# Expert 0's gated output as the accumulator's first value, and the forms of x on VectorE alone

## The chip, the core and the metric

The kernel runs on one core of a Trainium2 chip. TensorE does the matrix products, VectorE and ScalarE read the product banks (PSUM) and write SBUF, GpSimd works from SBUF to SBUF and also issues some transfers, SyncE issues the other transfers. Each engine takes its instructions strictly in the order in which they stand in its queue. The metric is the device time of one launch in microseconds; the median of three runs counts.

## The reference

A recurrent attention gives x (3072 tokens of 384 features). A mixture of 8 experts with a Sinkhorn-normalised gate P follows, and a small gated network after that.

```
P = exp(x @ w_gate - max); 8 times: P /= P.sum(1); P /= P.sum(0); P *= N / E
for e in range(E):
    h = np.maximum(x @ w1[e], 0.0)
    out += P[:, e:e + 1] * (h @ w2[e])
x = out
return ((x @ m1) * (x @ m2)) @ w3 @ w_out
```

The change lies in the sum over the experts: in how the term of expert 0 comes into `out`.

## The kernel before, in words

**Stages.** From 0 to about 430 us the attention runs, and beside it the whole of expert 0 (its raw output, without the gate, goes to DRAM as `y0_d`, three slices `kk` of 128 features each). From there to about 1753 us run experts 1 to 7 in three **passes** of two chunks `s` of 512 tokens. Then comes the gated network. A pass has 14 **units** (expert `e_`, half `h` of its hidden features).

**A unit** (`unit`) has first products and second products. The first products make the hidden features of two pairs `q` of slices by a scheme with 7 multiplications in place of 8 (`STEPS`); their moving operands are not x itself but nine **forms** of it, sums and differences of x's blocks, each split in a high and a low part (`fm(j, 0)`, `fm(j, 1)`, kept in tiles `xT` and `xr`). ScalarE holds partial products in the four buffers `rt` (`hold`), VectorE adds them back into the bank (`done`, rows `b<-b,rt`), ScalarE and VectorE make the high and low part of the positive part (`relu`, tiles `hA`, `hB`). The second products fill six banks, chunk 1 before chunk 0, three slices each; VectorE multiplies each bank by the gate (`tmp<-b,pb`), and GpSimd adds the result to `acc` (six accumulators of 128x512). In the first unit of a pass, (1, 0), VectorE writes `acc` directly.

**Forms** (`forms`). At the end of a pass x of the next two chunks lies in a region of `xT`. ScalarE makes nine high parts; nine low parts (`form`) and four differences (`diff`) are made by VectorE or GpSimd, whichever a planner takes. The differences lie in the four `rt` buffers too.

**Expert 0's term** (`add_first`). At unit (4, 0) of each pass the gate of expert 0 is loaded into an `rt` buffer per chunk, six slices of `y0_d` into the two `tmp` buffers in turn, GpSimd or VectorE multiplies, GpSimd adds to `acc`.

**Beside it** run the loads of the weights (`wA`, `wS`, issued by GpSimd in passes 1 and 2; in pass 0 they are formed from raw weights), and the conversion of the last network's weights (`convert`, tiles `cv`, `cvr`), lowest in priority, on all three vector engines, with loads and stores on SyncE's queue. After a pass `acc` is stored to `xf_d`.

**What sets the order.** Every operation is entered in a list with its priority, cost and dependences, and a planner (`Plan.order`) lays them out in advance on a time line of its own estimates; each engine's queue then follows that line, and no engine steps past a waiting instruction.

Of the kernel before, what the change touches and what calls it, by code (L numbers as in the profile page):

```python
# [334 lines left out]
class Kernel:  # L335
# [634 lines left out]
    def forms(self, p, prio):  # L970
# [22 lines left out]
        def diff(y, a, b, r):  # L993
            g.op(both, lambda e: self.tt(e, tv[y](), a(), b(), ALU.subtract), r=rk + r, w=[t[y]], prio=prio)
# [15 lines left out]
    def unit(self, p, e_, h, pr, pe, pb):  # L1010
# [75 lines left out]
        for s in (1, 0):  # L1086
            bl = [(M[q][3]["12" if s else "11"], M[q][4]) for q in range(2)] + [(M[q][3]["22" if s else "21"], M[q][4] + 1) for q in range(2)]
            pbv = lambda s=s: T["pb"][:, pb[s].at]
            for kk in range(3):
                y = self.psum.new("yb")  # L1090

                def m2(e, y=y, kk=kk, bl=tuple(bl)):
                    o = self.ps(y, 512)
                    for x, (hh, b) in enumerate(bl):
                        hv = self.hv(hh)
                        wh, wl = self.w2(b, 0, kk), self.w2(b, 1, kk)
                        self.mm(o, wh, hv[:, 0], start=(x == 0), stop=False)
                        self.mm(o, wl, hv[:, 0], start=False, stop=False)
                        self.mm(o, wh, hv[:, 1], start=False, stop=(x == 3))
                g.op({"PE": 12 * .229}, m2, r=[(hh, i, 0) for hh, b in bl for i in range(2)] + [("w", b % 8, i) for hh, b in bl for i in range(2)],  # L1100
                     w=[y], prio=pr + .1 + .01 * (3 * (1 - s) + kk))
                av = lambda s=s, kk=kk: T["acc"][:, s, kk]
                ak = ("acc", s, kk)
                if e_ == 1 and h == 0:
                    g.op({"DVE": dveb(512)}, lambda e, y=y, av=av, pbv=pbv: self.tt("DVE", av(), self.ps(y, 512), pbv(), ALU.mult),
                         r=[y, pb[s]], w=[ak], prio=pe)
                else:
                    tm = self.tmpring.new()
                    tv = lambda tm=tm: T["tmp"][:, tm.at]
                    g.op({"DVE": dveb(512)}, lambda e, y=y, tv=tv, pbv=pbv: self.tt("DVE", tv(), self.ps(y, 512), pbv(), ALU.mult),  # L1110
                         r=[y, pb[s]], w=[tm], prio=pe)
                    g.op({"POOL": pool2(512)}, lambda e, tv=tv, av=av: self.tt(e, av(), av(), tv(), ALU.add),
                         r=[tm], w=[ak], prio=pe)
# [3 lines left out]
    def add_first(self, p, pr):  # L1117

        nc, g, T = self.nc, self.g, self.T
        for s, ch in enumerate(self.PASSES[p]):  # L1120
            b = self.rt.new()
            bv = lambda b=b: T["rt"][:, b.at]
            self.dma(bv, lambda ch=ch: T["p_d"][0, 512 * ch:512 * ch + 512].partition_broadcast(128), 262144, ["pd"], [b], pr)
            for kk in range(3):
                tm = self.tmpring.new()
                tv = lambda tm=tm: T["tmp"][:, tm.at]
                self.dma(tv, lambda ch=ch, kk=kk: T["y0_d"][kk, :, 512 * ch:512 * ch + 512], 262144,
                         [("y0", 2 * ch + st, kk) for st in range(2)], [tm], pr)
                g.op({"POOL": pool2(512), "DVE": BB * dveb(512, True)}, lambda e, tv=tv, bv=bv: self.tt(e, tv(), tv(), bv(), ALU.mult), r=[b], w=[tm], prio=pr)
                av = lambda s=s, kk=kk: T["acc"][:, s, kk]  # L1130
                g.op({"POOL": pool2(512)}, lambda e, tv=tv, av=av: self.tt(e, av(), av(), tv(), ALU.add), r=[tm],
                     w=[("acc", s, kk)], prio=pr)

    def phase_b(self):
# [31 lines left out]
        for n, (p, e_, h) in enumerate(units):  # L1166
# [7 lines left out]
            if (e_, h) == (1, 0):  # L1174
                self.forms(p, pr - .6)
            if h == 0:
                pb = [self.pbring.new() for _ in range(2)]
                for s in range(2):
                    self.dma(lambda s=s, pb=pb: T["pb"][:, pb[s].at], lambda s=s, e_=e_, p=p: T["p_d"][
# [7 lines left out]
            if (e_, h) == (4, 0):  # L1187
                self.add_first(p, pr + .6)
            if (e_, h) == (7, 1) and p < 2:
                for s, ch in enumerate(self.PASSES[p]):  # L1190
                    self.dma(lambda ch=ch: T["xf_d"][ch], lambda s=s: T["acc"][:, s], 786432, [("acc", s, kk) for kk in range(3)], [("xf", ch)], 260 + n / 100)

    def spread_p(self):
# [23 lines left out]
        self.after("pd", [g.wr["pd", i] for i in range(2)], -200, hook=free)  # L1217

# [54 lines left out]
    def phase_c(self):  # L1273
# [48 lines left out]
        self.after("yfree", self.e0_ops + [g.wr["lgr", c] for c in range(NCH)], 2999, hook=lambda end: outr.free.extend([(end, i) for i in range(2)]))  # L1322
# [3 lines left out]
        for ci, c in enumerate((5, 4, 0, 1, 2, 3)):  # L1326
# [5 lines left out]
            if ci > 1:  # L1332
                self.dma(xs, lambda c=c: T["xf_d"][c], 786432, [("xf", c)], ak, pc - 1.5)
# [158 lines left out]
```

## Time and profile before

| | us |
|---|---|
| median of three runs | 2114.1 (2111.39 to 2123.24) |
| the profiled execution, its own time | 2105.79 |
| its span, first to last instruction | 2104.0 |
| TensorE busy | 2025.7 |
| VectorE busy | 1230.1 |
| GpSimd busy | 847.2 |
| ScalarE busy | 708.2 |

Busy time is the union of an engine's instructions. "Idle before" in a row is the time that an engine stood still ahead of an instruction, and the name behind the arrow is what ended it. The granted clock of TensorE is 1.00 at 2.4 GHz and 0.50 at 1.2 GHz.

### The profile page before, as it was taken

Reading aid. Unit: us, or ns where it says so; the run is one execution under the profiler, and the core shown is the slowest. Engines: PE = TensorE matmul, PEld = TensorE weight load, DVE = VectorE, ACT = ScalarE, POOL = GpSimd, SP = SyncE. Lnnn points to the kernel's source line nnn. Section 1 sums busy time; section 2 is a strip of 40 time slices with the busy share of each in tenths; the row PEclk is TensorE's granted clock in tenths of the full one; section 3 lists DMA queues with packets and bytes.
Section 4 is the critical chain, followed back from the end, with each engine's and each line's share of the span. In section 5 each row is a group of like instructions: output and inputs, shape, how many; then the busy total and the mean of one; then the engine's idle time right before and its main releaser. Section 6 shows DMA issues by size and latency. Waiting matters only on the chain.

```text
span 2104.0 us, 39081 instructions
## 1 busy us (share of the span) xinstructions
PE 2025.7 (96%) x16017; PEld 1731.0 (82%) x16017; DVE 1230.1 (58%) x1935; ACT 708.2 (34%) x1355; POOL 847.2 (40%) x891
## 2 busy tenths in 40 slices
PE   2899999999999999999999999999999999999999
PEld 1799889988887888788887887888877888988888
DVE  7998883554535535766767767576677543222222
ACT  3543333243433433423322324223333222222222
POOL 3111101257668767544456455344564534200000
PEclk9899999999999999999999999999999999999999
DMA  6533333175546546655555545646555446410000
GB/s 218 163 88 109 94 101 106 56 267 207 194 177 227 186 183 232 235 194 212 210 201 187 192 149 192 235 166 209 194 197 210 157 139 192 99 46 16 16 18 28
DMA packets 165458, 331.57 MB, mean 158 GB/s; under 512 B 13280, under 2 KB 117664, under 8 KB 153760
## 3 DMA queue, kind: packets, MB, share of 16 engines
q1 hardware_dynamic: 131392, 193.82, 27.5%
q0 software_dynamic: 33888, 135.28, 18.7%
q8 instruction: 125, 2.05, 0.4%
q14 instruction: 53, 0.43, 0.1%
HBM read 235.10 MB, written 93.95 MB: 156 GB/s over the span
## 4 chain that ended last, share of the span: by engine, by line
PE 75%; DVE 3%; DMA 2%; issue 1%; POOL 1%; ACT 1%; SPq 0%; DVEq 0%; POOLq 0%; ACTq 0%
PE b L357 75%; DMA wA<-wq_d 1%; DMA wo_d<-cv 1%; DVE cv L371 1%; DVE xr L368 0%; DVE b L368 0%; POOL acc L368 0%; POOL cv L368 0%; DVE hA L371 0%; DMA rawB<-in_moe_w 0%; POOL tmp L368 0%; POOL wA L368 0%; ACT rt L361 0%; DVE tmp L368 0%; DMA w_d<-cv 0%
## 5 line engine op out<-in xcount | busy, mean ns | idle before, releaser
L357 PE MATMUL b<-hA,wA 128*128 128x512 f32 (+1 forms) x2367 | 504.6, 353 | 3.5 <-DVE hA L371 3.5
L357 PEld LDWEIGHTS b<-hA,wA 128*128 128x128 f32 x2367 | 391.1, 189 | 65.9 <-DVE hA L371 4.3
L368 POOL TENSOR_TENSOR acc<-acc,tmp 128x512 f32<-128x512 f32 x252 | 330.2, 1313 | 178.2 <-DVE tmp L368 176.7
L357 PE MATMUL b<-hB,wA 128*128 128x512 f32 x1521 | 388.3, 390 | 0.0
L357 PEld LDWEIGHTS b<-hB,wA 128*128 128x128 f32 x1521 | 286.4, 188 | 60.0 <-DVE hB L371 0.4
L357 PE MATMUL b<-xr,wA 128*128 128x256 f32 (+1 forms) x1620 | 328.8, 336 | 3.3 <-DVE xr L368 3.1
L368 DVE TENSOR_TENSOR tmp<-b,pb 128x512 f32<-128x512 f32 x234 | 161.2, 689 | 231.6 <-PE b L357 211.6
L357 PEld LDWEIGHTS b<-xr,wA 128*128 128x128 f32 x1620 | 250.6, 190 | 36.7 <-DVE xr L368 3.5
L361 ACT ACTIVATE rt<-b 128x512 f32<-128x512 f32 x300 | 178.0, 597 | 247.1 <-PE b L357 238.9
L357 PE MATMUL b<-xT,wA 128*128 128x512 f32 x1008 | 250.7, 389 | 0.6 <-DMA wA<-wq_d 0.6
L368 DVE TENSOR_TENSOR b<-b,rt 128x512 f32<-128x512 f32 x252 | 173.2, 695 | 110.8 <-ACT rt L361 69.8
L357 PEld LDWEIGHTS b<-xT,wA 128*128 128x128 f32 x1008 | 188.9, 188 | 40.8 <-DMA wA<-wq_d 1.4
L368 POOL TENSOR_TENSOR cv<-cv 128x256 f32<-128x256 f32 (+3 forms) x171 | 124.9, 730 | 197.7 <-DVE cv L1254 114.3
L357 PE MATMUL b<-xT,wS 128*128 128x512 f32 x756 | 199.5, 390 | 4.6 <-ACT rt L361 4.6
L371 DVE SCALAR_TENSOR_TENSOR hA<-b,hA 128x512 fp32r<-128x512 f32 x215 | 144.3, 687 | 67.3 <-ACT hA L1060 40.8
L357 PEld LDWEIGHTS b<-xT,wS 128*128 128x128 f32 x756 | 141.5, 188 | 35.9 <-ACT rt L361 6.7
L368 DVE TENSOR_TENSOR rt<-b,rt 128x512 f32<-128x512 f32 x48 | 33.2, 692 | 186.0 <-PE b L357 186.0
L1060 ACT ACTIVATE hB<-b 128x512 fp32r<-128x512 f32 x169 | 100.4, 595 | 96.6 <-DVE b L368 94.7
L371 DVE SCALAR_TENSOR_TENSOR hB<-b,hB 128x512 fp32r<-128x512 f32 x169 | 115.0, 684 | 26.4 <-ACT hB L1060 26.0
L361 ACT ACTIVATE cv<-cv 128x256 fp32r<-128x256 f32 x72 | 29.1, 404 | 284.9 <-DVE cv L371 284.9
L1060 ACT ACTIVATE hA<-b 128x512 fp32r<-128x512 f32 x167 | 97.6, 596 | 47.6 <-DVE b L368 26.1
L368 POOL TENSOR_TENSOR wA<-rawB,wA 128x768 fp32r<-128x768 f32 (+1 forms) x53 | 91.1, 1729 | 31.8 <-ACT wA L361 27.2
(175 smaller groups left out, 2355.9 us busy)
## 6 DMA issues: line engine op xcount, KB each, us to landing
wA<-wq_d POOLq DMA_DIRECT2D x56, 1536.0 KB, 9.0
wq_d<-wA SPq DMA_DIRECT2D x28, 1536.0 KB, 7.0
wS<-ws_d POOLq DMA_DIRECT2D x56, 512.0 KB, 4.9
rawB<-in_moe_w SPq DMA_DIRECT2D x108, 192.0 KB, 3.1
ws_d<-wS SPq DMA_DIRECT2D x28, 512.0 KB, 3.2
w_d<-cv SPq DMA_DIRECT2D x112, 128.0 KB, 1.8
pb<-p_d SPq DMA_DIRECT2D x42, 256.0 KB, 3.8
cvr<-in_w3T SPq DMA_DIRECT2D x32, 256.0 KB, 2.7
```

The lines of the kernel that those rows point to most:

```text
L357: self.nc.tensor.matmul(*args, skip_group_check=True, **kw)
L361: self.nc.scalar.activation(out=out, in_=in_, func=AF.Copy, **({} if scale is None else {"scale": scale}))
L368: self.E[eng].tensor_tensor(out=out, in0=in0, in1=in1, op=op)
L371: self.nc.vector.scalar_tensor_tensor(out=out, in0=in0, scalar=scalar, in1=in1, op0=op0, op1=op1)
L1060: g.op({"ACT": actb(512)}, lambda e: nc.scalar.activation(out=hv(0), in_=self.ps(s, 512), func=AF.Relu), r=[s], w=[(out, 0, 0)], prio=pe)
```

## The change

`add_first` is gone. A new `first` runs at the start of a pass, ahead of unit (1, 0): per chunk it loads the gate of expert 0 into a buffer of the ring `pb`, loads the slices of `y0_d` straight into `acc`, and VectorE multiplies `acc` by the gate in place. Unit (1, 0) then goes through `tmp` and GpSimd's addition like every other unit. The ring `pb` has a third buffer, which lies in `yr` (expert 0's output tile, free after expert 0). The forms' low parts and differences are VectorE's alone. The store of `acc` after a pass is cut into six of 256 KB, one for each slice, so that a slice's load can follow its own store.

```diff
-        both = {"POOL": pool2(512), "DVE": dveb(512, True)}
+        dve_ = {"DVE": dveb(512)}
...
-            g.op(both, lambda e: self.tt(e, four(self.fm(j, 1)), src(), four(self.fm(j, 0).bitcast(F32)), ALU.subtract),
+            g.op(dve_, lambda e: self.tt("DVE", four(self.fm(j, 1)), src(), four(self.fm(j, 0).bitcast(F32)), ALU.subtract),
...
-            g.op(both, lambda e: self.tt(e, tv[y](), a(), b(), ALU.subtract), r=rk + r, w=[t[y]], prio=prio)
+            g.op(dve_, lambda e: self.tt("DVE", tv[y](), a(), b(), ALU.subtract), r=rk + r, w=[t[y]], prio=prio)
...
-                if e_ == 1 and h == 0:
-                    g.op({"DVE": dveb(512)}, lambda e, y=y, av=av, pbv=pbv: self.tt("DVE", av(), self.ps(y, 512), pbv(), ALU.mult),
-                         r=[y, pb[s]], w=[ak], prio=pe)
-                else:
-                    tm = self.tmpring.new()
...
-    def add_first(self, p, pr):
...
+    def first(self, p, pr):
+
+        g, T = self.g, self.T
+        pb = [None, None]
+        for s in (1, 0):
+            ch = self.PASSES[p][s]
+            b = pb[s] = self.pbring.new()
+            bv = lambda b=b: self.pv(b)
+            self.dma(bv, lambda ch=ch: T["p_d"][0, 512 * ch:512 * ch + 512].partition_broadcast(128), 262144, ["pd"], [b], pr)
             for kk in range(3):
...
+                self.dma(av, lambda ch=ch, kk=kk: T["y0_d"][kk, :, 512 * ch:512 * ch + 512], 262144,
+                         ["bopen"] + [("y0", 2 * ch + st, kk) for st in range(2)], [("acc", s, kk)], pr)
+                g.op({"DVE": dveb(512)}, lambda e, av=av, bv=bv: self.tt("DVE", av(), av(), bv(), ALU.mult), r=[b], w=[("acc", s, kk)], prio=pr)
...
+            if (e_, h) == (1, 0):
+                self.first(p, pr - .5)
...
-            if (e_, h) == (4, 0):
-                self.add_first(p, pr + .6)
...
-                for s, ch in enumerate(self.PASSES[p]):
-                    self.dma(lambda ch=ch: T["xf_d"][ch], lambda s=s: T["acc"][:, s], 786432, [("acc", s, kk) for kk in range(3)], [("xf", ch)], 260 + n / 100)
+                for s in (1, 0):
+                    ch = self.PASSES[p][s]
+                    for kk in range(3):
+                        self.dma(lambda ch=ch: T["xf_d"][ch, :, kk], lambda s=s, kk=kk: T["acc"][:, s, kk], 262144, [("acc", s, kk)],
+                                 [("xf", ch, kk)], 260 + n / 100)
```

The planner lays out the rest anew. Three places follow, all at the change from pass 0 to pass 1; `b` is a product bank, the names are those above.

VectorE during the first products of unit (7, 1). Before:

```order
L371 SCALAR_TENSOR_TENSOR hB<-b_137,hB 128x512
L371 SCALAR_TENSOR_TENSOR hB<-b_135,hB 128x512
L368 TENSOR_TENSOR b_134<-b_134,rt 128x512
L368 TENSOR_TENSOR b_139<-b_139,rt 128x512
L368 TENSOR_TENSOR xr<-xT,xr 128x512
L371 SCALAR_TENSOR_TENSOR hB<-b_134,hB 128x512
L371 SCALAR_TENSOR_TENSOR hA<-b_139,hA 128x512
L371 SCALAR_TENSOR_TENSOR hA<-b_141,hA 128x512
L371 SCALAR_TENSOR_TENSOR hA<-b_136,hA 128x512
```

The same place now:

```order
L371 SCALAR_TENSOR_TENSOR hB<-b_135,hB 128x512
L371 SCALAR_TENSOR_TENSOR hB<-b_138,hB 128x512
L368 TENSOR_TENSOR b_137<-b_137,rt 128x512
L368 TENSOR_TENSOR b_134<-b_134,rt 128x512
L368 TENSOR_TENSOR rt<-xT,rt 128x512
L371 SCALAR_TENSOR_TENSOR hB<-b_137,hB 128x512
L371 SCALAR_TENSOR_TENSOR hA<-b_141,hA 128x512
L371 SCALAR_TENSOR_TENSOR hA<-b_134,hA 128x512
L371 SCALAR_TENSOR_TENSOR hA<-b_136,hA 128x512
L368 TENSOR_TENSOR xT<-xT 128x512
L368 TENSOR_TENSOR xT<-rt,xT 128x512 x2
L368 TENSOR_TENSOR xr<-xT,xr 128x512
```

One operation of the forms stands between the last `done` and the `relu` rows in both; the low part `xr` has moved behind the `relu` rows, together with what was GpSimd's.

VectorE from the fourth gate product of unit (7, 1) into unit (1, 0) of pass 1, now (before, no row on `acc` stood here):

```order
L368 TENSOR_TENSOR tmp<-b_141,pb 128x512
L371 SCALAR_TENSOR_TENSOR cv<-cv 128x256
L368 TENSOR_TENSOR acc<-acc,pb 128x512
L368 TENSOR_TENSOR tmp<-b_134,pb 128x512
L368 TENSOR_TENSOR tmp<-b_136,pb 128x512
L368 TENSOR_TENSOR b_135<-b_135,rt 128x512
L1251 TENSOR_SCALAR cv<-cvr 128x256
L368 TENSOR_TENSOR b_138<-b_138,rt 128x512
L371 SCALAR_TENSOR_TENSOR hB<-b_135,hB 128x512
L368 TENSOR_TENSOR acc<-acc,pb 128x512
L371 SCALAR_TENSOR_TENSOR hA<-b_138,hA 128x512
L368 TENSOR_TENSOR acc<-acc,pb 128x512
```

The first product of `first` stands between the fourth and the fifth gate product of unit (7, 1), the next two among the `done` and `relu` rows of unit (1, 0).

SyncE's queue at the same place. Before:

```order
L388 DMA xT<-xs_d 128x6x128 x4
L388 DMA cvr<-in_moe_w 128x512
L388 DMA w_d<-cv 128x256 x2
L388 DMA pb<-p_d 128x512
L388 DMA xf_d<-acc 128x1536
```

Now:

```order
L388 DMA xf_d<-acc 128x512
L388 DMA xT<-xs_d 128x6x128 x4
L388 DMA acc<-y_d 128x512
L388 DMA xf_d<-acc 128x512
L388 DMA yr<-p_d 128x512
L388 DMA xf_d<-acc 128x512
L388 DMA cvr<-in_moe_w 128x512
L388 DMA w_d<-cv 128x256
L388 DMA xf_d<-acc 128x512
L388 DMA w_d<-cv 128x256
L388 DMA acc<-y_d 128x512 x2
```

`acc<-y_d` is the load of expert 0's slice; the first stands behind the four loads of the next pass's x (`xT<-xs_d`), the second and third behind the store of a converted weight (`w_d<-cv`).

## Rows read from the trace of the kernel before

**Rows 1.** The page's first part: busy time, share of the span, instructions.

```profile
PE 2025.7 (96%) x16017; PEld 1731.0 (82%) x16017; DVE 1230.1 (58%) x1935; ACT 708.2 (34%) x1355; POOL 847.2 (40%) x891
```

**Rows 2.** Busy table: stretch, length, busy PE, PEld, DVE, ACT, POOL, granted clock.

```profile
651.00:667.00 16.00, 13.34 (x58) 10.39 (x58) 6.98 (x10) 7.24 (x14) 13.48 (x11) 1.00 0.41 125
...
851.00:863.00 12.00, 8.91 (x39) 7.08 (x39) 11.12 (x10) 8.38 (x16) 10.42 (x10) 1.00 0.35 127
863.00:1105.00 242.00, 242.00 (x1069) 200.35 (x1069) 163.66 (x273) 76.33 (x146) 116.41 (x131) 1.00 0.60 212
1105.00:1148.00 43.00, 38.84 (x167) 30.40 (x165) 33.99 (x49) 13.88 (x28) 28.16 (x28) 1.00 0.53 174
...
1302.00:1312.00 10.00, 6.51 (x28) 5.08 (x27) 9.93 (x9) 6.44 (x13) 8.03 (x7) 0.97 0.41 141
...
1555.00:1598.00 43.00, 38.59 (x166) 30.51 (x165) 33.59 (x46) 14.14 (x28) 29.92 (x30) 1.00 0.51 176
```

**Rows 3.** TensorE's waits from 360 us on: total us, times, longest.

```profile
PE b L357 <- ACT rt L361: 11.0, 10, 2.1
PE b L357 <- DVE xr L368: 4.0, 2, 3.1
PE b L357 <- DVE hA L371: 3.5, 1, 3.5
```

**Rows 4.** Instructions on tile rt: ns shortest/median/longest, first and last start.

```profile
L368 POOL TENSOR_TENSOR tmp<-tmp,rt x18: 1277/1294/1360, 657.6 to 1574.8; 128x512 f32<-128x512 f32 x18
...
L388 SPq DMA_DIRECT2D rt<-p_d x6: 319/320/978, 630.1 to 1525.1; - x6
...
L368 DVE TENSOR_TENSOR xr<-rt,xr x4: 676/680/1466, 432.3 to 1315.8; 128x512 fp32r<-128x512 f32 x4
```

**Rows 5.** Timeline at the change to pass 1: VectorE, then GpSimd, then TensorE.

```profile
856.22 5.97 DVE L368 TENSOR_TENSOR xr<-xT,xr 128x512 fp32r<-128x512 f32 x1
...
856.66 1.28 POOL L368 TENSOR_TENSOR rt<-xT 128x512 f32<-128x512 f32 x1
857.91 2.51 POOL L368 TENSOR_TENSOR xT<-xT 128x512 fp32r<-128x512 f32 x2
860.39 1.25 POOL L368 TENSOR_TENSOR rt<-xT,rt 128x512 f32<-128x512 f32 x1
...
862.25 0.73 PE L357 MATMUL b<-xr,wA 128*128 128x512 f32 x2 [3.09 <-DVE xr L368]
```

**Rows 6.** The same table as rows 2, behind the wait at pass 2.

```profile
1311.40:1314.70 3.30, 3.30 (x10) 2.54 (x9) 2.93 (x7) 0.00 (x0) 0.31 (x1) 0.50 0.34 123
```

**Rows 7.** Transfers issued from 860 to 875 us: count, KB each, us to landing.

```profile
xT<-xs_d SPq DMA_DIRECT2D x4, 384.0 KB, 6.1
xf_d<-acc SPq DMA_DIRECT2D x1, 768.0 KB, 4.1
```

**Rows 8.** The same from 878 to 900 us.

```profile
wA<-wq_d POOLq DMA_DIRECT2D x2, 1536.0 KB, 11.8
...
xf_d<-acc SPq DMA_DIRECT2D x1, 768.0 KB, 14.7
...
pb<-p_d SPq DMA_DIRECT2D x1, 256.0 KB, 5.1
w_d<-cv SPq DMA_DIRECT2D x2, 128.0 KB, 13.6
```

**Rows 9.** All issues of the page's kind: mid-pass loads of expert 0's slices.

```profile
tmp<-y_d SPq DMA_DIRECT2D x18, 256.0 KB, 3.2
```

**Rows 10.** Timeline at the start of pass 0: GpSimd, then VectorE.

```profile
429.87 3.38 POOL L368 TENSOR_TENSOR wA<-rawB,wA 128x768 fp32r<-128x768 f32 x2 [1.08 <-ACT wA L361]
433.21 3.87 POOL L368 TENSOR_TENSOR wA<-acc,wA 128x768 fp32r<-128x768 f32 x2
...
433.73 1.92 DVE L368 TENSOR_TENSOR wA<-sums,wA 128x128 fp32r<-128x128 f32 x1
435.57 0.69 DVE L368 TENSOR_TENSOR b<-b,rt 128x512 f32<-128x512 f32 x1
```

More of the change, by code (lines that the diff above doesn't have):

```diff
@@ L1087, in unit @@
             bl = [(M[q][3]["12" if s else "11"], M[q][4]) for q in range(2)] + [(M[q][3]["22" if s else "21"], M[q][4] + 1) for q in range(2)]
-            pbv = lambda s=s: T["pb"][:, pb[s].at]
+            pbv = lambda s=s: self.pv(pb[s])
             for kk in range(3):
@@ L1115 @@
-    STEPS = [(q, s) for ss in ((0, 1), (2, 3), (4,), (5,), (6,)) for q in range(2) for s in ss]
-    def add_first(self, p, pr):
-        nc, g, T = self.nc, self.g, self.T
-        for s, ch in enumerate(self.PASSES[p]):
-            b = self.rt.new()
-            bv = lambda b=b: T["rt"][:, b.at]
+                tm = self.tmpring.new()
+                tv = lambda tm=tm: T["tmp"][:, tm.at]
+                g.op({"DVE": dveb(512)}, lambda e, y=y, tv=tv, pbv=pbv: self.tt("DVE", tv(), self.ps(y, 512), pbv(), ALU.mult),
+                     r=[y, pb[s]], w=[tm], prio=pe)
@@ L1123, in add_first @@
+                g.op({"POOL": pool2(512)}, lambda e, tv=tv, av=av: self.tt(e, av(), av(), tv(), ALU.add),
+                     r=[tm], w=[ak], prio=pe)
+    STEPS = [(q, s) for ss in ((0, 1), (2, 3), (4,), (5,), (6,)) for q in range(2) for s in ss]
+    def first(self, p, pr):
[5 more added lines that the diff above has]
+            bv = lambda b=b: self.pv(b)
             self.dma(bv, lambda ch=ch: T["p_d"][0, 512 * ch:512 * ch + 512].partition_broadcast(128), 262144, ["pd"], [b], pr)
@@ L1124, in add_first @@
             for kk in range(3):
[L1125 to L1129, printed above, removed]
                 av = lambda s=s, kk=kk: T["acc"][:, s, kk]
-                g.op({"POOL": pool2(512)}, lambda e, tv=tv, av=av: self.tt(e, av(), av(), tv(), ALU.add), r=[tm],
-                     w=[("acc", s, kk)], prio=pr)
+                self.dma(av, lambda ch=ch, kk=kk: T["y0_d"][kk, :, 512 * ch:512 * ch + 512], 262144,
+                         ["bopen"] + [("y0", 2 * ch + st, kk) for st in range(2)], [("acc", s, kk)], pr)
@@ L1186, in phase_b @@
                 self.after("cv0", [g.wr["acc", 0, 2]], 2)
-            if (e_, h) == (4, 0):
-                self.add_first(p, pr + .6)
             if (e_, h) == (7, 1) and p < 2:
-                for s, ch in enumerate(self.PASSES[p]):
-                    self.dma(lambda ch=ch: T["xf_d"][ch], lambda s=s: T["acc"][:, s], 786432, [("acc", s, kk) for kk in range(3)], [("xf", ch)], 260 + n / 100)
+                for s in (1, 0):
+                    ch = self.PASSES[p][s]
+                    for kk in range(3):
+                        self.dma(lambda ch=ch, kk=kk: T["xf_d"][ch, :, kk], lambda s=s, kk=kk: T["acc"][:, s, kk], 262144, [("acc", s, kk)],
+                                 [("xf", ch, kk)], 260 + n / 100)
     def spread_p(self):
@@ L1217, in spread_p, with pv @@
         self.after("pd", [g.wr["pd", i] for i in range(2)], -200, hook=free)
+        self.after("yrfree", self.e0_ops + [g.wr["lgr", c] for c in range(NCH)], -200, hook=lambda end: self.pbring.free.append((end, 2)))
+    def pv(self, b):
+        return self.T["pb"][:, b.at] if b.at < 2 else self.T["yr"].rearrange("p s n -> p (s n)")[:, 0:512]
     def hv(self, h, part=0, n=512):
@@ L1321, in phase_c @@
         outr = Ring([])
-        self.after("yfree", self.e0_ops + [g.wr["lgr", c] for c in range(NCH)], 2999, hook=lambda end: outr.free.extend([(end, i) for i in range(2)]))
+        self.after("yfree", self.e0_ops + [g.wr["lgr", c] for c in range(NCH)] + [g.wr["acc", s, kk] for s in range(2) for kk in range(3)], 2999, hook=lambda end: outr.free.extend([(end, i) for i in range(2)]))
         self.after("tmpfree", [g.wr["acc", s, kk] for s in range(2) for kk in range(3)], 2999,
@@ L1332, in phase_c @@
             if ci > 1:
-                self.dma(xs, lambda c=c: T["xf_d"][c], 786432, [("xf", c)], ak, pc - 1.5)
+                self.dma(xs, lambda c=c: T["xf_d"][c], 786432, [("xf", c, kk) for kk in range(3)], ak, pc - 1.5)
             ak = ak + ["x5free"]
```

7 lines of the change are left out of this document (1 added, 6 removed).

## The prediction, made before the changed kernel ran

> **What bounds the kernel now.** I read the page's first part, then the busy table by stretch, then TensorE's list of waits, then the timeline at each wait. TensorE is busy for 96% of the span [rows 1], so a change pays only where TensorE stands still, and no saving on another engine counts by itself. In the stretch of a whole run of units, 863 to 1105 us, it does not stand still at all: 242.00 us busy of 242.00 for 1069 matmuls, 0.226 us each [rows 2]. It stands still in five short stretches: 16.00 - 13.34 = 2.66 us at 651, 43.00 - 38.84 = 4.16 at 1105, 43.00 - 38.59 = 4.41 at 1555, and 12.00 - 8.91 = 3.09 at 851, 10.00 - 6.51 = 3.49 at 1302 [rows 2]. That is 11.2 us in three stretches and 6.6 in two, 17.8 in all. Behind the last one there are 3.3 us in which the granted clock is 0.50, that is 1.2 GHz [rows 6]; half of that, 1.7 us, is lost too. So 19.5 us, 0.9% of the time, is all that lies within this change's reach.
>
> **What the change removes.** The three long stretches lie where `add_first` runs: its six loads of the gate into `rt` start between 630.1 and 1525.1 us, its 18 multiplications on GpSimd (1.29 us each) between 657.6 and 1574.8 [rows 4]. Two of four `rt` buffers are then taken, and TensorE's largest wait is for ScalarE's writes to `rt`, 11.0 us in 10 times [rows 3]. Units that do not share `rt` with it run without a gap [rows 2]. I take the 11.2 us as gone. The two short stretches are the changes of pass. There VectorE's low part `xr<-xT,xr` took 5.97 us for work that takes 0.68 [rows 4, 5]: GpSimd ran four further operations of the forms in that time, from 856.66 to 861.64, without a gap, and VectorE got through behind the last one. TensorE waited 3.09 us for it [rows 5] and 3.49 at the next pass for the `hA` part queued behind the like instruction [rows 2, 3]. With the forms off GpSimd that row of four does not exist; the 6.6 us and the slow clock behind them, 1.7 us, go. Removed: 11.2 + 6.6 + 1.7 = 19.5 us.
>
> **What it adds to VectorE.** At a change of pass the forms have thirteen operations of this kind, nine low parts and four differences, of which GpSimd made most (four of them in rows 5). Were it all of them, 13 x 0.68 = 8.8 us would come to VectorE [rows 4], and six products of `first` at the same 0.68, 4.1 us. From the order: ahead of the second products only one form stands between the last `done` and the `relu` rows, as before; with 0.69 us a row the first `relu` that the second products need is done about 1 us before TensorE asks for it, so I cost the forms themselves at nothing. Their cover is the 2.72 us (12 matmuls of 0.226) between two gate products, of which VectorE uses 0.69. The conversion rows share that time but come last in priority. GpSimd loses 18 multiplications and gains no addition, since the six additions of unit (1, 0) replace six of mid-pass. That is idle time off the path.
>
> **What it adds in waits.** This is the open part. Nothing in the trace shows an in-place product that waits for a load, so I bound it by rows. M is the start of the second products of the last unit of a pass; bank k of six is full at M + 2.72 k, its gate product done 0.9 us later, GpSimd's addition after 1.3 more.
>
> Change to pass 1. The first slice's store goes out at M + 5 and lands by M + 9.1 (4.1 us for three times the bytes [rows 7]). The load waits for that and stands behind the four loads of x, 1.5 MB at 6.1 us each [rows 7], which start when the last form has read the old x, about M + 6.6. I put its landing at M + 17. VectorE reaches its product at M + 12 and waits 5 us; queued behind it are the fifth and sixth gate products, and nobody needs their banks before the next unit's second half. TensorE goes on. The cost comes next: the second and third load stand in SyncE's queue behind the store of a converted weight, whose low part GpSimd makes after the fifth addition, so after that wait. They are issued near M + 20.7, together with the weight loads of 1.5 MB. Beside such loads a 256 KB load landed in 5.1 us, stores in 13.6 and 14.7 [rows 8]; alone it is 3.2 [rows 9]. VectorE gets to the second product at M + 21.4, among the `done` and `relu` rows of unit (1, 0), and is released between M + 26 and M + 31 (5.1 us after the issue, or twice that). TensorE is through its second products at M + 16.3 and through sixteen groups of three matmuls at M + 27.2; there it wants the `done` behind that product, and has it between M + 28 and M + 33; the first product of chunk 0 then stands once more among the `relu` rows (0 to 3 us). Bounds 1 to 9 us; I take 5, a middle, since the nearest row (5.1) is a load issued first and these are issued just after.
>
> Change to pass 2. Here no x is loaded ahead, the store of the converted weight stands before the second load, and by the same count the load goes out at M + 20.3, some 1.5 us before the weights. VectorE waits about 2 us where it has as much to spare; 1 us, bounds 0 to 5.
>
> Start of pass 0. GpSimd makes weights without a gap from 429.87 to 437.08 us, and a VectorE row of 128 elements took 1.92 us beside it [rows 10]. The new three products and one more form, 0.68 us each, come ahead of the `done` that started at 435.57 [rows 10], and the gate that they need comes some 2 us later, since three more forms stand between the Sinkhorn steps on VectorE. TensorE followed that `done` with almost no slack. Bounds 1 to 6 us; I take 3.
>
> Clock: a wait of 3.49 us was followed by the low level once [rows 2, 6]; a wait of 5 at pass 1 may be. 1.7 us, bounds 0 to 3.4.
>
> **Two rules weighed.** The row shows that VectorE waited through four GpSimd instructions [rows 5]. The Trainium skill (SBUF — State Buffer, section "Who interferes with whom") says that a VectorE instruction with two SBUF inputs contends with a GpSimd instruction that reads SBUF, and that whichever issues second is blocked until the first has finished, which would be one instruction. The trace agrees on who contends and not on how long. By that rule the start of pass 0 would cost at most 2 us and the sum come out 1 us lower; by the row up to 6. The second rule makes a result of its own, and stands with the first rival.
>
> **The rivals.**
> - Loads get through. If a 256 KB load beside the weight loads takes 5.1 us as in rows 8 or less, VectorE is back before TensorE asks: pass 0 costs 1, pass 1 costs 1, no slow clock: -19.5 + 2 = -17.5, 2096.6 us. For it: that row. Against it: in rows 8 the stores beside it took over 13. The Trainium skill (DMA: Bandwidth & Descriptors, section "Queues, rings and completion order") has each DMA engine take turns between queues packet by packet; by that a small load in SyncE's queue would never wait for a large one in GpSimd's to end, and this is the case that follows. The 13.6 and 14.7 us of the stores speak against it as the whole story.
> - Loads are as slow as the stores. All upper bounds: 6 + 9 + 5 + 3.4 = 23.4; -19.5 + 23.4 = +3.9, 2118 us, no change.
> - VectorE's place becomes the bound (slower). Each product of `first` waits in VectorE's order for a load that waits for a store, under the weight loads. A store of 14.7 and a load of 10 (twice 5.1) is 25 us, 10 of which VectorE has at most; 15 us at each of two changes of pass are 30, with 3 at pass 0 and 3.4 of clock: -19.5 + 36.4 = +17, 2131 us. It decides once the waits sum to 30 us. Against it: the first store goes out before the weight loads, in the clear.
> - The change does not do what it says: mid-pass waits stay, since `hold` waits for VectorE's `done` and not for the buffers that `add_first` takes. Then 11.2 us are not gained: -8.8 + 11.2 = +2.4, 2116.5 us. Against it: runs of units without it show no gap.
>
> **How the numbers follow.** Forecast: -19.5 + 5 + 1 + 3 + 1.7 = -8.8 us. The profiled execution took 2105.79 us, 1.8 over its span, and would come to 2097; the median of the runs is 8.3 us above that execution, so I set the difference against the median: 2114.1 - 8.8 = 2105.3 us. Its own range is 2100 to 2111. About 0.5% (10.6 us) is what a measurement of this kernel can tell from no change. Chances: forecast 0.44 (of it 0.17 beyond 0.5% faster, 0.27 within), loads get through 0.24, loads slow 0.15, VectorE the bound 0.12, mid-pass waits stay 0.05. Faster by over 0.5%: 0.17 + 0.24 = 0.41; within: 0.27 + 0.15 + 0.05 = 0.47; slower 0.12. The range reaches from 2095, within the first rival, to 2120, above the second, and leaves out the slower case and the outer part of the first.
>
> **What will show it.** Right: in mid-pass units TensorE has no wait for `rt`; at the changes of pass no VectorE row of 5 us beside GpSimd; VectorE's rows `acc<-acc,pb` and `acc<-acc,yr` have idle time before them that ends with `acc<-y_d`, about 5 us each at pass 1 for the first two, and TensorE's next wait, about 5 us, follows there for a `done`. Wrong: a TensorE wait in second products of unit (7, 1), waits of over 10 us at a change of pass, or `acc<-y_d` landing within 4 us throughout.

## The result, and the profile after

The changed kernel takes 2092.7 us (median of 6 runs, 2087.3 to 2099.7) against 2113.3 us for the kernel before (6 runs on the same chip): ratio 0.9897, 95% interval 0.9865 to 0.9928, 20.6 us less. The forecast was 2105.3 us with a range from 2095 to 2120; the time lies 2.3 us below that range. The profiled execution took 2087.25 us, its span is 2085.4 (before 2105.79 and 2104.0).

The page's first part, after [rows 1]: TensorE's work is the same and its share of the span 97%; GpSimd lost 43 us of work and VectorE gained 6.

```profile
PE 2021.4 (97%) x16017; PEld 1732.8 (83%) x16017; DVE 1236.4 (59%) x1970; ACT 709.9 (34%) x1355; POOL 804.4 (39%) x856
```

The largest of TensorE's waits from 360 us on, after (engine, what it waited for: total us, times, longest) [rows 3]. The 11.0 us for `rt` are 2.1, the longest wait is 1.4 us.

```profile
PE b L357 <- DVE hA L371: 2.5, 2, 1.4
PE b L357 <- ACT rt L361: 2.1, 3, 1.0
PE b L357 <- POOL wA L368: 1.2, 1, 1.2
PE b L357 <- DVE xr L368: 0.9, 1, 0.9
```

The busy table over the places of the old stalls, after (stretch, length, busy PE, ...) [rows 2]: TensorE fills every one of them; the 1.1 us missing in the long row from 858 us on are a new wait, at 891 us.

```profile
647.00:663.00 16.00, 16.00 (x72) 13.26 (x71) 5.01 (x8) 5.87 (x10) 9.91 (x8) 1.00 0.22 72
858.00:1098.00 240.00, 238.91 (x1054) 197.61 (x1053) 163.00 (x273) 76.07 (x144) 123.39 (x133) 1.00 0.61 210
1098.00:1141.00 43.00, 43.00 (x191) 35.63 (x190) 28.88 (x53) 17.16 (x33) 17.74 (x22) 1.00 0.63 218
1292.00:1300.00 8.00, 8.00 (x37) 6.60 (x37) 7.79 (x14) 4.58 (x9) 1.16 (x2) 1.00 0.52 186
1540.00:1582.00 42.00, 42.00 (x187) 34.80 (x186) 28.30 (x50) 16.31 (x32) 18.34 (x22) 1.00 0.62 218
```

**Where the time went, place by place.** Both traces hold the same 16,017 matmuls, so the start of the n-th in one can be set against the start of the n-th in the other; how much that difference grows over a stretch is what the stretch gained or lost. "Forecast" is the terms of the prediction's sum that belong to the stretch.

| stretch (us in the kernel before) | forecast | after | forms alone | first alone | late loads | later products, two executions |
|---|---|---|---|---|---|---|
| 360 to 425, end of attention | 0 | -1.5 | -1.5 | +3.6 | -0.6 | -1.2, -1.8 |
| 425 to 500, start of pass 0 | +3 | +2.4 | 0.0 | +2.1 | +2.8 | +1.0, +0.7 |
| 640 to 700, mid-pass 0 | -2.7 | -3.3 | 0.0 | -3.3 | -3.3 | -3.3, -3.3 |
| 845 to 900, change to pass 1 | -3.1 + 5 | -2.0 | -3.4 | 0.0 | +8.7 | -3.4, -3.4 |
| 1090 to 1165, mid-pass 1 | -4.2 | -5.7 | +1.0 | -5.7 | -5.7 | -5.7, -5.7 |
| 1230 to 1260 | 0 | -0.8 | +0.6 | -0.8 | -0.8 | -0.8, -0.8 |
| 1295 to 1380, change to pass 2 | -5.2 + 1 | -2.6 | -5.4 | +5.0 | -2.8 | -4.6, -4.8 |
| 1540 to 1610, mid-pass 2 | -4.4 | -5.8 | +0.6 | -5.8 | -5.8 | -5.8, -5.8 |
| clock, anywhere | +1.7 | 0 | | | | |
| 360 to 1760, sum | -8.8 | -19.2 | -7.6 | -4.4 | -7.4 | -23.8, -24.7 |

Stretches left out are within 0.5 us. The last four columns are experiments. In all of them but the late loads the planner lays out every queue anew, so that places which an edit does not touch can differ too.

**The change to pass 1, after.** VectorE's timeline (start us, us, engine, line, operation, [idle before <- releaser]). The first product of `first` waited 1.85 us for its slice, the second and third not at all, the fourth (chunk 0, `yr`) 3.93 us, with three `relu` rows on `hA` behind it.

```profile
872.29 0.69 DVE L368 TENSOR_TENSOR acc<-acc,pb 128x512 f32<-128x512 f32 x1 [1.85 <-DMA acc<-y_d]
...
878.13 0.67 DVE L368 TENSOR_TENSOR acc<-acc,pb 128x512 f32<-128x512 f32 x1
...
879.33 0.67 DVE L368 TENSOR_TENSOR acc<-acc,pb 128x512 f32<-128x512 f32 x1
...
890.04 0.69 DVE L368 TENSOR_TENSOR acc<-acc,yr 128x512 f32<-128x512 f32 x1 [3.93 <-DMA acc<-y_d]
890.65 1.88 DVE L371 SCALAR_TENSOR_TENSOR hA<-b,hA 128x512 fp32r<-128x512 f32 x3
```

The transfers issued from 872.9 to 874.9 us and from 874.9 to 884.5 us (count, KB each, median us to landing) [rows 7, 8]: the same 256 KB load takes 3.6 us in the first two microseconds and 13.1 behind the weight loads.

```profile
acc<-y_d SPq DMA_DIRECT2D x2, 256.0 KB, 3.6
...
wA<-wq_d POOLq DMA_DIRECT2D x2, 1536.0 KB, 11.7
...
acc<-y_d SPq DMA_DIRECT2D x2, 256.0 KB, 13.1
```

GpSimd's timeline there, then SyncE's. The low part of the converted weight (871.54) stands ahead of the fifth addition (873.72), which waits for VectorE; the weight load follows at 874.95. SyncE issues the second and third load before that, from 872.98 us on.

```profile
870.05 1.53 POOL L368 TENSOR_TENSOR acc<-acc,tmp 128x512 f32<-128x512 f32 x1
871.54 0.73 POOL L368 TENSOR_TENSOR cv<-cv 128x256 fp32r<-128x256 f32 x1
873.72 1.29 POOL L368 TENSOR_TENSOR acc<-acc,tmp 128x512 f32<-128x512 f32 x1 [1.46 <-DVE tmp L368]
874.95 0.57 POOL L388 DMA_DIRECT2D wA<-wq_d  x1
...
872.98 1.54 SPq L388 DMA_DIRECT2D acc<-y_d  x2
```

### The profile page after: what moved, and what is told of

Same layout as the page of the kernel before. It is cut to its first block, busy times and chain, and to the rows that moved or that the text cites. A ratio compares the mean times of both kernels' runs of the same rounds, so it can differ in the third digit from the quotient of the medians.

```text
span 2085.4 us, 39076 instructions
## 1 busy us (share of the span) xinstructions
PE 2021.4 (97%) x16017; PEld 1732.8 (83%) x16017; DVE 1236.4 (59%) x1970; ACT 709.9 (34%) x1355; POOL 804.4 (39%) x856
## 4 chain that ended last, share of the span: by engine, by line
PE 88%; DVE 4%; issue 4%; DMA 2%; POOL 1%; ACT 0%; SPq 0%; POOLq 0%; DVEq 0%; ACTq 0%
PE b L357 88%; DMA acc<-y_d 1%; DVE prod L368 1%; DMA kt<-in_kT 1%; DVE t L568 0%; DMA rawB<-in_moe_w 0%; POOL wA L368 0%; SPq L388 0%; DVE xs L568 0%; POOL sums L368 0%; DVE asys L602 0%; DVE asys L542 0%; DVE nrm L471 0%; DVE cv L368 0%; DVE cv L371 0%
## 5 line engine op out<-in xcount | busy, mean ns | idle before, releaser
L368 POOL TENSOR_TENSOR acc<-acc,tmp 128x512 f32<-128x512 f32 x252 | 335.9, 1335 | 196.8 <-DVE tmp L368 194.5
L368 POOL TENSOR_TENSOR cv<-cv 128x256 f32<-128x256 f32 (+3 forms) x179 | 131.7, 736 | 204.7 <-DVE cv L1255 112.3
L368 DVE TENSOR_TENSOR tmp<-b,pb 128x512 f32<-128x512 f32 x150 | 103.3, 690 | 138.5 <-PE b L357 134.3
L368 DVE TENSOR_TENSOR tmp<-b,yr 128x512 f32<-128x512 f32 x102 | 70.3, 690 | 111.2 <-PE b L357 103.3
```

The lines of the kernel that those rows point to most:

```text
L368: self.E[eng].tensor_tensor(out=out, in0=in0, in1=in1, op=op)
```

## Experiments

### Each part of the change alone

The kernel before with the forms on VectorE alone:

```diff
-        both = {"POOL": pool2(512), "DVE": dveb(512, True)}
+        both = {"DVE": dveb(512)}
```

> The kernel before with one part of the change: the forms' low parts and differences are VectorE's alone; expert 0's term is still added in mid-pass. Theory: the gains add up by place. Compared matmul by matmul, the changed kernel gained 3.4 us at the change to pass 1 and 5.4 at the change to pass 2 (with the half clock there), and 15.6 in the three mid-pass stretches. This kernel has the first two and not the third: about -8 us, ratio 0.996 (0.994 to 0.998); mid-pass waits of TensorE for rt stay at about 11 us in the list of waits. At the start of pass 0, where the changed kernel lost 2.4 us, it loses under 1, since no product of expert 0 stands there. Rival: GpSimd's four operations only happened to stand there, and VectorE with all thirteen forms is late by itself: TensorE still waits 2 to 3 us at each change of pass, ratio 0.999 to 1.002.

Measured: ratio 0.9951 (0.9933 to 0.9970). The two changes of pass gave 3.4 and 5.4 us, and TensorE has no wait there; the mid-pass stretches lost 0 to 1 us (in the one that lost 1.0 the granted clock was 0.50 from 1142.99 to 1146.40 us). TensorE's list of waits begins:

```profile
PE b L357 <- ACT rt L361: 11.1, 9, 2.6
```

The rival falls: thirteen forms on VectorE make nobody late.

The other part alone (the forms of the changed kernel free for both engines again):

```diff
-        dve_ = {"DVE": dveb(512)}
+        dve_ = {"POOL": pool2(512), "DVE": dveb(512, True)}
...
```

> The other part alone: expert 0's products at the start of a pass, straight in the accumulator, as in the changed kernel; the forms free for GpSimd or VectorE as before. Theory: the mid-pass stretches give their 15.6 us; at the changes of pass a VectorE operation of the forms again sits beside a row of GpSimd operations for 5 us or more and TensorE waits 3 to 5 us each time; in-place products add 1 to 3 us a pass as in the changed kernel. About -8 us in all, ratio 0.996 (0.993 to 0.998). Rival: the waits at the changes of pass came from where the mid-pass work pushed GpSimd's queue, and go with it: then both parts are not needed and this kernel is as fast as the changed one, ratio 0.990.

Measured: ratio 0.9979 (0.9959 to 1.0000), at the upper end of what the theory gave. The mid-pass stretches gave all of theirs. VectorE's row of 6 us is back at the change to pass 1; at the change to pass 2 a product of `first` waited 6.20 us, and TensorE's waits there (second fence, 1300 to 1390 us) are the old 3.5 for `hA` and a new 3.0 for `b`.

```profile
860.12 5.99 DVE L368 TENSOR_TENSOR xr<-xT,xr 128x512 fp32r<-128x512 f32 x1
...
1337.99 0.69 DVE L368 TENSOR_TENSOR acc<-acc,yr 128x512 f32<-128x512 f32 x1 [6.20 <-DMA acc<-y_d]
```

```profile
PE b L357 <- DVE hA L371: 3.5, 1, 3.5
PE b L357 <- DVE b L368: 3.0, 1, 3.0
PE b L357 <- ACT rt L361: 1.5, 1, 1.5
```

So the two parts remove different stalls, and the rival falls: the waits at the changes of pass did not go with the mid-pass work. Their sums, 7.6 and 4.4, come 7.2 us short of 19.2. Half of that, 3.6 us, lies between 365 and 376 us, in the attention, where TensorE's granted clock was 0.50 for 6.8 us in this execution and in none of the others, behind a wait of 1.01 us for ScalarE (0.29 before); the parts of the change do not explain it. The busy table of that stretch (granted clock third from the right; it was 1.00 before):

```profile
365.00:376.00 11.00, 9.07 (x50) 8.16 (x49) 2.43 (x3) 2.79 (x6) 2.84 (x5) 0.71 0.31 119
```

Most of the rest is 2.2 us at the change to pass 2, where `first` alone pays more for its loads, and 2.2 us that the forms alone lose from mid-pass 1 on.

### Forms on GpSimd alone: who is held up

```diff
-        both = {"POOL": pool2(512), "DVE": dveb(512, True)}
+        both = {"POOL": pool2(512)}
```

> The kernel before with all of the forms' low parts and differences on GpSimd. Theory: VectorE's 5.97 us came from an operation with two SBUF inputs (the low part xr) that met a row of GpSimd operations; what VectorE does at a change of pass besides reads one bank and one SBUF tile (relu, done, gate products, 0.69 us each) and goes through beside GpSimd. So no VectorE row over 2.5 us at the changes of pass and no wait of TensorE for VectorE's hA there. What may come instead: GpSimd's thirteen operations of 1.28 us take 16.6 us, its additions queue behind them, and TensorE waits for a form or a tmp buffer; where that stays under 3 us the kernel gains 3 to 8 us, ratio 0.996 to 0.999. Rival: VectorE's rows with one bank input are held up by GpSimd's row just as long, then rows of 3 us or more on hA, hB or b stand at both changes and TensorE's waits there stay at 3 us each or grow, ratio 1.000 or above.

Measured: ratio 0.9979 (0.9957 to 1.0002). At pass 2 the stall is gone (-5.3), at pass 1 it is larger (+3.6): TensorE waits 4.3 us for `hB`, and the granted clock is 0.50 from 867.65 to 874.48 us. From 360 to 1760 us this execution is 1.8 us longer than the kernel before, as the theory gave a gain only where the new wait stays under 3 us. VectorE's timeline at pass 1, then GpSimd's:

```profile
859.52 1.28 DVE L371 SCALAR_TENSOR_TENSOR hB<-b,hB 128x512 fp32r<-128x512 f32 x2
860.72 1.28 DVE L368 TENSOR_TENSOR b<-b,rt 128x512 f32<-128x512 f32 x2
861.92 6.82 DVE L1254 TENSOR_SCALAR cv<-cv 128x256 int32<-128x256 int32 x1
868.66 0.68 DVE L371 SCALAR_TENSOR_TENSOR hB<-b,hB 128x512 fp32r<-128x512 f32 x1
```

```profile
859.86 1.31 POOL L368 TENSOR_TENSOR rt<-xT,rt 128x512 f32<-128x512 f32 x1
861.12 1.30 POOL L368 TENSOR_TENSOR xT<-rt,xT 128x512 fp32r<-128x512 f32 x1
...
867.33 1.25 POOL L368 TENSOR_TENSOR xr<-rt,xr 128x512 fp32r<-128x512 f32 x1
```

Rows with a bank among their inputs go through beside GpSimd in their usual time (two of them in 1.28 us, twice), as the theory had it, and the rival falls. But the theory's "no row over 2.5 us" falls as well: a conversion with one SBUF input, which takes 0.29 us elsewhere, took 6.82, from inside one GpSimd operation to the end of the fifth one after it, with the urgent `hB` row behind it. At pass 2 another one took 5.36 us beside such a row, and there an `hA` row stood behind it without making TensorE wait. The Trainium skill (SBUF — State Buffer, section "Who interferes with whom") names `tensor_scalar` among the operations that can take the ports which VectorE shares with GpSimd, and this row agrees; by the same section the one that comes second waits until the first is finished, and here, as in rows 5, it waited through the whole row of them.

### What the mid-pass waits were

The kernel before with expert 0's gate in a third buffer of `pb` (in `yr`) instead of `rt`:

```diff
-            b = self.rt.new()
-            bv = lambda b=b: T["rt"][:, b.at]
+            b = self.pbring.new()
+            bv = lambda b=b: self.pv(b)
...
```

> The kernel before with one buffer moved: in mid-pass the gate of expert 0 goes into a third buffer of the ring pb (in yr) and no longer into one of the four rt buffers. The 18 multiplications, the loads into tmp and the additions stay. Theory: TensorE stood in mid-pass because two of four rt buffers were taken: its waits for rt fall from 11.0 us to under 3, and 12 to 15 us are gained, ratio 0.993 to 0.995. Rival: it stood because the slices of expert 0 took the tmp buffers and GpSimd's time, and VectorE's gate products (and with them the banks) waited: then TensorE still waits 8 us or more in the three stretches, whatever it is put down to, and the ratio is 0.998 to 1.000.

Measured: ratio 1.0000 (0.9984 to 1.0016). The waits for `rt` went, as the theory said, and others came, as the rival said: by place -3.3, +1.2 and +1.8 us. The last two hold a stretch at half clock behind the new wait (granted clock 0.50 from 1137.53 to 1140.94 and from 1588.09 to 1594.92 us); half of what lies behind the waits is about 1.7 and 2.6 us. TensorE's list:

```profile
PE b L357 <- DVE tmp L368: 7.0, 2, 4.0
...
PE b L357 <- ACT rt L361: 1.7, 4, 0.6
```

One third buffer had brought a wait of its own: the second gate was loaded only when the first was used up, and GpSimd's multiplications waited for it (2.0 us). So each gate got a place of its own, in `rawB`, in passes 1 and 2, and is loaded after an addition of unit (3, 1):

```diff
-            b = self.rt.new()
-            bv = lambda b=b: T["rt"][:, b.at]
+            b = ("g0", s) if p else self.rt.new()
+            bv = (lambda s=s: T["rawB"][:, s, 0:512]) if p else lambda b=b: T["rt"][:, b.at]
...
+            if (e_, h) == (3, 1):
+                self.after(("gdep", p), [g.wr["acc", 1, 0]], 2)
```

> The kernel before; in passes 1 and 2 the two gates of expert 0 for add_first lie in the raw-weight tile rawB, which is idle by then, each in a place of its own, and take no rt buffer; pass 0 is untouched. With one shared third buffer the waits for rt went, but the second gate was then loaded only after the first was used up, the tmp buffers were held meanwhile and TensorE waited 3.0 and 4.0 us for VectorE's gate products. Theory: the waits in mid-pass are the taken rt buffers and nothing else: the stretches of passes 1 and 2 give 5.7 us each, as in the changed kernel, the one of pass 0 nothing, -11.5 us in all, ratio 0.994 to 0.996. Rival: expert 0's slices in the two tmp buffers are a second limit of their own, and behind the rt waits TensorE waits for tmp all the same: less than half of the 11.5 us, ratio 0.997 to 1.000.

Measured: ratio 0.9964 (0.9936 to 0.9991). By place mid-pass 1 gave 2.8 and mid-pass 2 gave 1.9 us, 4.7 of the 11.5: the rival, though not by much. Behind the wait for `tmp` in mid-pass 2 (1.79 us) nine matmuls took 3.81 us in place of 2.04, with the granted clock at 0.50; without that, which a wait of this length does not always bring, it would be 6.5 of 11.5. The two changes of pass lost 1.5 and 1.2 us here, where such stretches follow the old waits too, so that from 360 to 1760 us only 1.0 us is gained. The busy table's row, TensorE's waits, then GpSimd's and VectorE's timelines in mid-pass 1:

```profile
1594.32:1597.73 3.41, 3.41 (x9) 2.27 (x8) 2.70 (x4) 0.54 (x2) 3.41 (x3) 0.50 0.43 146
```

```profile
PE b L357 <- ACT rt L361: 4.1, 5, 1.4
...
PE b L357 <- DVE tmp L368: 3.4, 2, 1.8
```

```profile
1142.60 1.33 POOL L368 TENSOR_TENSOR tmp<-tmp,rawB 128x512 f32<-128x512 f32 x1
1144.01 5.31 POOL L368 TENSOR_TENSOR acc<-acc,tmp 128x512 f32<-128x512 f32 x4
```

```profile
1144.00 0.68 DVE L368 TENSOR_TENSOR tmp<-b,pb 128x512 f32<-128x512 f32 x1
```

VectorE's first gate product of the unit starts when GpSimd's last multiplication of expert 0 ends (1143.93): until then its slices hold the two `tmp` buffers. Mid-pass thus had two limits, one behind the other: `rt` and, some microseconds later, `tmp` with GpSimd's chain. Of the kernels run here only those without the mid-pass work are rid of both.

### The loads of the second and third slice, behind the weight loads

The changed kernel; at the change to pass 1 two loads move in SyncE's queue, nothing moves on VectorE (`late` holds the loads of chunk 1, slices 1 and 2; `stores` is the last store of `acc` of pass 0):

```diff
+        for o, m in self.late:
+            order.remove(o)
+        i = order.index(self.stores) + 1
...
+        order[i:i] = [o for o, m in self.late]
```

> The changed kernel with two instructions moved in SyncE's queue: at the change to pass 1 the second and third load of expert 0's slices are issued behind the last store of the accumulator, some 4 us later, and so after GpSimd's weight loads instead of before them (872.98 and 874.20 us in the changed kernel, the first weight load at 874.95). VectorE's order is untouched. This is the order that the forecast had in mind. Theory: what saved the changed kernel there was the place in the queue; a load issued behind the weight loads takes about 14 us (the fourth did, issued at 875.92), so these land near 891, VectorE stands for some 12 us at the second product, with five done rows and four relu rows of the same unit behind it, and TensorE loses 7 to 11 us in this stretch in place of 1.4. Ratio to the kernel before 0.993 to 0.996. Rival: the forecast's price, 5.1 to 10 us a load, holds and TensorE loses 1 to 6 us. Second rival: VectorE has so much to spare there that the place doesn't matter, and TensorE loses no more than 2.5 us.

Measured: ratio 0.9938 (0.9911 to 0.9966). The stretch loses 8.7 us where the changed kernel gained 2.0, so the place in the queue is worth 10.7 us, and the loads cost 12.1 us where they cost 1.4 (both against the forms alone), 1 us more than the theory's upper end; both rivals fall. TensorE's wait is 9.84 of it, and about 2 us are the half clock behind that wait. The transfers issued from 880 to 885 us, VectorE's row, and TensorE's timeline:

```profile
wA<-wq_d POOLq DMA_DIRECT2D x2, 1536.0 KB, 11.7
acc<-y_d SPq DMA_DIRECT2D x3, 256.0 KB, 13.7
```

```profile
896.67 0.69 DVE L368 TENSOR_TENSOR acc<-acc,pb 128x512 f32<-128x512 f32 x1 [12.80 <-DMA acc<-y_d]
```

```profile
899.89 1.65 PE L357 MATMUL b<-xr,wA 128*128 128x512 f32 x3 [9.84 <-DVE b L368]
901.34 1.48 PE L357 MATMUL b<-xT,wA 128*128 128x512 f32 x3
```

Behind the wait three matmuls take 1.48 us where they take 0.84 at the full clock. The three loads landed at 895.58, 896.65 and 897.25 us, the second weight load at 895.40. The transfers from 883 to 890 us by queue (packets as the trace counts them, MB, share) suggest why they end together. GpSimd's queue (`software`) and SyncE's (`hardware`) moved nearly as many packets, but of 11.3 and 1.9 thousand bytes, so the weights got 2.02 MB and the small loads 0.29.

```profile
q0 software_dynamic: 179, 2.02, 81.0%
q1 hardware_dynamic: 154, 0.29, 17.3%
```

The Trainium skill (DMA: Bandwidth & Descriptors, section "Queues, rings and completion order") lets the queues take turns packet by packet. The near-equal counts agree with that, if a packet of the trace is one of the page's, which no run here shows. Equal turns are then not equal shares: the small loads had a seventh of what the weights had.

### The products later in VectorE's order

The changed kernel, with the remaining waits as the target: the planner is told that the loads of chunk 0 land 14 us later, so that their products come behind the `relu` rows, and at pass 0 the products come behind the making of the weights.

```diff
-                         ["bopen"] + [("y0", 2 * ch + st, kk) for st in range(2)], [("acc", s, kk)], pr)
+                         ["bopen"] + [("y0", 2 * ch + st, kk) for st in range(2)], [("acc", s, kk)], pr, lat=14.0 if p and not s else 0.0)
-                g.op({"DVE": dveb(512)}, lambda e, av=av, bv=bv: self.tt("DVE", av(), av(), bv(), ALU.mult), r=[b], w=[("acc", s, kk)], prio=pr)
+                g.op({"DVE": dveb(512)}, lambda e, av=av, bv=bv: self.tt("DVE", av(), av(), bv(), ALU.mult), r=[b] + ([] if p else ["made1"]), w=[("acc", s, kk)], prio=pr)
...
+                self.after("made1", g.ops[m:-3], -200)
```

> The changed kernel with VectorE's order altered at three places: at pass 0 the products of expert 0 come behind the making of the weights, and at passes 1 and 2 the three products of chunk 0 stand later (the planner is given 14 us more for their loads), behind the relu rows of unit (1, 0). Theory: in the changed kernel TensorE lost 1.25 us at pass 1 and 1.6 at pass 2 because relu rows stood in VectorE's queue behind a product whose load took 14 us beside the weight loads, and 2.2 at pass 0 because products and GpSimd's making of weights slowed each other. With the products out of the way 2 to 4 us of these 5 go: 2083 to 2085 us for a profiled execution of 2087, and no relu row waits behind acc<-y_d. Rival: the loads land too late in any order, the products then hold up GpSimd's additions and tmp buffers, and TensorE waits as long at another place: no gain, ratio to the kernel before as the changed one (0.990) or above.

Measured: ratio 0.9880 (0.9861 to 0.9899). The profiled execution took 2094.6 us and not 2083 to 2085, since its first 360 us, the attention, took 12.1 us more than the changed kernel's. By place 4.6 us less than the changed kernel from 360 us on: 1.4 at pass 0, 1.4 at pass 1, where the chunk 0 product no longer stands ahead of the `hA` rows, and 2.1 at pass 2. There the expectation named the wrong product: it is the third of chunk 1 that waits, and it still stands ahead of them; VectorE did not wait for it here (4.62 us in the changed kernel): its load landed at 1336.43 us, just before VectorE came to it at 1336.98. It was then run once more, beside the changed kernel, on one chip:

> The changed kernel itself once more, beside the next run on the same chip. Theory: what differs between profiled executions of one program lies in the first 360 us, the attention (over the profiled kernels so far that stretch took 0.6 to 15 us more than in the kernel before, with no change to it); from 360 us to the end the trace repeats the first one within 0.5 us. Ratio to the kernel before 0.989 to 0.991. Rival: the differences come from places all over the span, and stretches after 360 us differ by over 1 us between two executions too.

> The changed kernel with the later products (as in the first run of it) once more, for a direct comparison. From 360 us on it took 4.6 us less than the changed kernel. Theory: the difference is real and shows in the medians: 2 to 7 us below the changed kernel's, ratio 0.986 to 0.989. Rival: the profile's 4.6 us are lost elsewhere in most executions, and the two medians agree within 1 us.

Measured: the changed kernel 2096.5 us, ratio 0.9900 (0.9872 to 0.9928); the later products 2090.1 us, ratio 0.9860 (0.9834 to 0.9886). The gain is real, 6.4 us between the medians, and this version beats both kernels. TensorE's whole list from 360 us on in the second execution begins:

```profile
PE b L357 <- DVE xr L368: 0.9, 1, 0.9
PE b L357 <- POOL wA L368: 0.7, 1, 0.7
```

The repeat of the changed kernel differs from the first by 1.4 us after 360 us, half of it at the start of pass 0 (3.1 against 2.4 us), which is more than the theory's 0.5; no place differs by over 1 us.

## Why the prediction was wrong, step by step

**Mid-pass, 11.2 us forecast, 14.8 measured** in the three stretches, and 0.8 at 1239 us. That all of it goes was right. The size was read wrongly from the busy table: the profile counts a group of matmuls as busy to the modelled end of the last one. Three matmuls show as 0.84 us and nine as 2.20, where matmuls in full flow start 0.226 apart (0.68 and 2.04), so each short stall shows 0.16 us too small and many short ones hide a good part. Counting would have found most of it in the same rows [rows 2]: 43.00 - 167 x 0.2264 = 5.2, 43.00 - 166 x 0.2264 = 5.4, 16.00 - 58 x 0.2264 = 2.9, together 13.5. The reason given (two of four `rt` buffers taken) was about half of it: 4.7 us of 11.5 in passes 1 and 2, 6.5 without the half clock of that execution. `tmp` was the other half.

**The two changes of pass, 6.6 + 1.7 forecast, 8.8 measured** (3.4 and 5.4, seen undisturbed in the forms alone). Right in mechanism and size.

**The forms on VectorE at no cost: right.** With the forms alone TensorE has no wait at the changes of pass.

**The added wait at pass 1, 5 us forecast, 1.4 measured, and the clock, 1.7 forecast, 0 measured: this step failed.** It said that the second and third load stand behind the store of a converted weight "whose low part GpSimd makes after the fifth addition", and so go out near M + 20.7, with the weight loads. M was 857.0 us. In GpSimd's queue the low part stands ahead of the fifth addition, one place earlier than the prediction has it. The loads went out at M + 15.9 and M + 17.2, before the weight loads at M + 17.9, and landed in 3.8 and 3.4 us; VectorE waited for neither. The first product waited 1.85 us and not 5. The price in that step was too low as well: with the loads where the forecast had put them, they take 13 to 14 us and not 5.1 to 10, and TensorE waits 9.84 us, above the upper bound of 9, with about 2 us of half clock behind it. Two errors of opposite sign, of which the first decided. With the loads there the ratio is 0.9938, some 2100 us: inside the forecast's range, but by luck, since the mid-pass gain was taken too small and this wait too short.

**The first rival** (2096.6 us, "a 256 KB load beside the weight loads takes 5.1 us or less") came nearest in number and is wrong in its reason: of the slices' loads issued behind a weight load at these two changes of pass, while the weights moved, the quickest took 10.3 us. Turns between queues agree with the rows (179 packets against 154), but they did not make the small loads quick.

**The added wait at pass 2, 1 us forecast, 2.8 measured** (bounds 0 to 5): the mechanism right, one load overlooked. The second load did go out ahead of the weights as forecast (1313.55 against 1314.25 us) and took 4.6 us; the third (1315.76) went out behind the first weight load, took 13.9 us, and the `hA` rows behind its product cost TensorE 1.41 us. A further 0.78 us is a wait for `rt`. At pass 1 it is the fourth product, the first of chunk 0, whose late load holds up `hA` and costs most of the 1.4 us; the prediction has that one, with 0 to 3 us.

**The start of pass 0, 3 us forecast, 2.4 measured:** right in size. VectorE's three products took 6.55 us there beside GpSimd's making of weights, but TensorE's two new waits are for a weight that GpSimd makes (`wA`, 1.19 us) and for `rt` (1.01), not for the `done`.

```profile
429.13 6.55 DVE L368 TENSOR_TENSOR acc<-acc,pb 128x512 f32<-128x512 f32 x3
```

**The end of the attention, 0 forecast, 1.5 gained,** with the forms alone too. It was not foreseen, and it is the stall of the changes of pass once more. In the kernel before, a row of GpSimd's forms ran from 395.98 to 404.33 us, and three of VectorE's steps of the gate beside it took 1.2 to 1.4 us where they take 0.36 without it (the first two lines before, the last after). TensorE waited 0.66 and 0.40 us for their result, `cs`. Both waits are in every kernel here that leaves forms to GpSimd, and in none that does not.

```profile
396.26 1.24 DVE L371 SCALAR_TENSOR_TENSOR p<-p,cs 128x192 f32<-128x192 f32 x1
...
399.94 0.39 PE L357 MATMUL b<-cs,ones 128*128 128x8 f32 x2 [0.66 <-DVE cs L953]
...
396.83 0.36 DVE L371 SCALAR_TENSOR_TENSOR p<-p,cs 128x192 f32<-128x192 f32 x1
```

In sum the forecast's -8.8 is -19.2: 4.4 from the mid-pass stretches, 5.3 from pass 1 and the clock, 0.5 from the changes of pass, 2.1 from 360 to 500 us, less 1.8 at pass 2.

## What to carry to other kernels

At one clock, a stall's size is the length of its stretch less the number of matmuls times their spacing, not less the busy time. Whether a small load is late is settled by its place against the large ones: read every queue that it and they stand in, row by row, and count what the price is on either side before choosing a middle. A row of GpSimd operations without a gap can hold up a VectorE operation with two inputs in SBUF (5.97 us for 0.68), or a conversion with one (6.82 for 0.29), and what stands behind it. Put nothing urgent behind such an operation there, or keep the kind of work on one engine. A measured stretch can hold a spell at half clock that another execution lacks: look at the granted clock before an edit is given the time.

## What the hardware showed besides

- Most of the difference between executions lies in the attention: of 5.5 us between the two traces of the changed kernel 4.3 are in the first 360 us. From 60 to 300 us the granted clock was 1.00 in the profiled execution of the changed kernel and 0.92 in that of the kernel with the gate in `rawB`, where the first 360 us, with the same work, took 14.9 us more than before. The first row is the changed kernel's busy table, the second that kernel's (the clock is the third figure from the right).

```profile
60.00:300.00 240.00, 230.60 (x5986) 211.94 (x5982) 217.97 (x360) 99.75 (x232) 27.16 (x21) 1.00 0.39 115
```

```profile
60.00:300.00 240.00, 225.82 (x5618) 207.12 (x5615) 206.59 (x338) 95.25 (x222) 26.17 (x21) 0.92 0.36 106
```

- The same 3.1 us wait at the change to pass 1 was followed by the full clock in the kernel before (it ended at 862.25 us) and in the kernel with `first` alone (866.16), and by 3.4 us at half of it in the two kernels with the gate moved (granted clock 0.50 from 867.88 and from 877.52 us): a wait of that length may or may not bring the low level.
